# A second order table for a kernel whose instruction order, engines and PSUM banks are read from a string

## The chip, the cores and the metric

The kernel runs on one core of a Trainium2 chip. The metric is the device time in microseconds (us) of one execution. A core has a matrix engine (TensorE, PE in the profile; its weight loads are listed as PEld), a vector engine (VectorE, DVE), a scalar engine (ScalarE, ACT), a general engine (GpSimd, POOL) and a queue engine (SyncE, SP) that here only issues DMAs. Each runs its own instructions in order and waits on semaphores for the others. PE writes its results to PSUM, eight banks of 512 fp32 numbers in each of 128 partitions; DVE and ACT take them from there.

## The reference

There are four batches of 6272 time steps with 256 channels. A gated recurrence is followed by a long convolution and two gates:

```python
# first layer
sig = 1 / (1 + exp(-f_logit))
f = lower_bound + (1 - lower_bound) * sig
for t in range(6272):
    h = f[:, t] * h + (1 - f[:, t]) * x[:, t]
    y[:, t] = h
# second layer, on x = y
x1, x2, x3 = split(x @ w_proj, 3)
conv = irfft(rfft(x2, axis=1) * rfft(filter_fft, axis=0))   # length 6272
out = (x1 * conv * x3) @ w_out
```

## The kernel before, in words

The convolution of length 6272 = 49 x 128 is done with matrix products: a first transform over the 128 (F1), a second over the 49 (F2), a product with the filter's spectrum, and the two inverse steps (I2, I1). The filter's own spectrum is made once, in the head of the program, and kept in DRAM (tile H).

The kernel does not emit instructions as its Python loops run. Each loop body registers operations with `plan.op` (class Plan, L62): a kind, the engines it may run on, what it reads and writes, and a function that emits it. At the end `plan.emit` goes through a table and emits the 2413 operations in the table's order. The table is the string ORDER (L125): three characters of a 64-letter alphabet are 18 bits, and they say which operation comes next, on which engine, and in which PSUM bank a matmul operation puts its result (L99 to L106). An assertion requires that every operation comes after those it depends on. So the order on every engine's queue, the choice of engine where there is one, and the banks are data, found by a search outside the kernel.

The kinds that matter here, with the lines under which the profile shows them:

- Head (batch 0 only). The filter is loaded in 13 pieces (L630), rounded for some (fr, copies on three engines), rotated by PE (rot, rot4, L645), copied out of PSUM (f2), transformed (FF1 L672, copies afs; FF2 L690, copies hw) and stored to H (hst, L699). Small tables come from a sine on ACT (L559), ten sign instructions (signs, L547 to L557, on POOL or DVE) and scalings of the weights (W, L484). Warm-up matmuls (L610) fill PE's waits.
- Recurrence, 13 chunks of 512 steps a batch. SP loads f_logit into FL and x into XT (load, L337; batches after the first reuse three buffers of each), ACT takes a sigmoid (sig, L340), POOL multiplies (u, L342), PE turns both halves (su, L354), ACT or DVE makes f (L367, L369), DVE scans (L375). The scan of a chunk needs that of the chunk before. A wrapped copy of the early steps (wrap: POOL or ACT, or a DMA, L299) prepares a rotation.
- Projection of x2: 13 P operations (L731), each one of eight matmuls of 256 columns (one has two), and as many copies out of PSUM (x2) by ACT (L289) or DVE (L294). P needs all scans of its batch; F1 needs all x2 copies.
- Spectrum, 16 units of 8 channels a batch: F1 (L744), its copy A, a small product at the edge (mini, L760, zm), F2 (L807), the product with the spectrum from H (loads L785 into four buffers). The product is either one DVE instruction straight from PSUM (L830, called MUL in the table) or a copy (prod, L289 or L294) with the product on POOL (L839). Then slot (POOL, L812), I2 (L849) and its copy Th.
- Gate: x1 and x3 projections, 52 x13 operations a batch (L403), their copies xs, and the product z, on DVE from PSUM (L424) or on POOL (L433).
- Output: I1 (L912), which needs all Th of the batch; y (DVE, L918), which needs all z; proj (L930), its copy o, and the store (L942). It shares its time with the recurrence of the next batch.

`copy` (L286) emits the copies on whichever engine the table names, so L289 and L291 are ACT's copies, L294 and L296 are DVE's, and L301 is POOL's, whatever the operation. The tiles in the profile tell them apart.

One batch follows the other as P, spectrum with gate, output; the recurrence of the next batch is mixed in from the late spectrum on.

Of the kernel before, what the change touches and what calls it, by code (L numbers as in the profile page):

```python
# [61 lines left out]
class Plan:  # L62
# [68 lines left out]
    "gAMYD1gChKEdYCeWF5gEJYETIEygEoACdECnSEWUCoCCfOCiYCjWEXECkGEUIEVYEeSEpYE9gCuQEfCEYME8gCvAEgKEhYEiWCwUFGgEjGEkOFHg"
    "CxECpQE0ACqACrYCzSC0KEqUErEElgEuWC+QFQgCsSEvGCVgEsMEwOCyYC/ADAQE1YB2gE+AE/YFRgDBAC5UCtKFIAE2WC6EE3OE4OFJYDDQDEAE"
    "5SFagE6CFbgC3UE7KC4EFAQFDWC7YFBAFCIFkgC8UDJSFSAC9EFlgDKCFKQClgFLADCYDQUDREExYEtgCmgFTYFNSFugFcADHUDIEFEOFFOFvgDO"
    "WDPGFMIFUQFOKFPKFVAFWIFmADGgENYEZgDXUFdYDMWFXSDNGFYKFZKDLYFeQDYECWgFfADTWFhUMpgFgIDUGDWgFnYDZSFoWFiEDaCFrQF4gDxY"
    "D9YDSYFpGFwAFxYMogFjMFsADeSDfCFqODFgDgUDhEFtIFyWFzGDcSF1UF2EF0OMRgEBAMQgDdCF3MDbYC1gDiYDjQDnWF6gDoGDkIDlgGPUGQEF"
    "9SGBQGCIMqAGJWGKGGFUGGMGLQGRWF+CGMAGSGF/SGDQGEAGHUGIMGNWGOOGACMSAF7QF8AGTSGUKJNUCFgDmgJPEJOVJQNJRYJSWJUGGXQGYIGZ"
    "SJTUJVsJXVC2gMTYGbWGaCJZFGcOGVQGWADVgJYSGfgJWYJaqGogGxgJbYG6gMcgJcTJdUJeDJhVJfsJgYJiQJjFJkoGdSGeKGgWGiuGjYGpUHFQ"
    "MdgGkGGlYJmXJnSGrsGhYHGAJoHJrTJtDGqYG7QG/AHNgJpqGyWG0GGsYGmTGtsGuYHDRG1YJsWJwVGnDG2uHfgHEBJuuGvTHAYJxRG9oG+YJyFG"
    "wDJ1SG3YJzpG8YGzYJ3CHHWJ2TJ4rJ5YHJUJ0YJ6QJ7RHIGJ8IJ9pJ+YG4SHKEHLUMeAMfYG5CHMMHPYHWgHOWHSuHXQHbAJ/UHBSHYYHcYHTYJv"
    "YKARKBEHogKEXHxUHCCHQuH7gHRYHZoIEgHaYKCJKDYKGHHyEHUSHhYHgWHkuHlYHiuINgHVCHjYKFQKHAKIYH1UH2EHdSHeCHpQHtoHuYHqYHro"  # L140
    "H3UH4EMrYHzWHmSH0GH8UHnCIAsH5QIBYH+EH6IIWgH/YMUWMVGH9YMWOMYSMZCIFUMaKM0gHsYHvQIHsIIYIGYM1gIJEIKYJlYIpgHwAKJVKLFI"
    "fWIgGJqYICQIPYIDAIygIOSISCITYIQqMgWMhGIhUIiMIXQILSIYYIbAIcYM2AI7gMiOM3YIMCIZoIaYKKRMkUNAgMlMIjWIRYIUSKMBKNYIkGIl"
    "QIVCImAMmMIqWIuuKOSKPTMbgInQIoIIrYKQCKRrKSYIdUI0YIsGItYIzWI1uI2YIeEI3GMsQIvYMtAMwSMuIMvYM4UNBgNMgKTWMxCNNgMyKI4Y"
    "KUXJEgM8QNZgNYgNCAKWHKYXM5EM6MKVGKXYM9AM+IIwSIxCI9YKZWJFUKaHKbuI8SJAqNOAKdXNDYKfHJJEI5QI6AJGYKeWKguJHEI+qKiXKjTK"
    "nVKpFKoWKquKkHNEQNFAKlrKmYNIUNGINJENKMI/YNigNjgKsSKtTKuCKvrKcYJIYNPYMngNaANbYJBYJCWJDGKxSKyQKzCKwYK0oK1YK2RK3UK4"
    "BK5sNQWNUSNsgNRGK6YNSOK7QK8RNtgNkALAULBVLFWMXgK9AK+pK/YJKYLCELDtLGXNcQNfULEYN2gNVCNWKLHGLIHLJYLKWLLXNdANeILMGLNv"
    "LOYNlYKhYN3gNgENhMKrYJLSJMCNLYRsWRtQLPSLQKRuGRvALUWNmQNHgNuAMjYLVONnANoINpUOAgOBgNqENrMLRSNvYLSCLTgLWWLeQLfILZSL"
    "aKLXGNwWNzUOLgOKgN4AN5YLYgNXANxGN0ENyOLgQN1MLhALigLbSLcCLdgOCAODYLjWLkORxQLoSLpKMzYN6URzAN9WOUgOVgN7EN8MN+GN/ONT"
    "YLlQLmAOMAONYLtSLuKOEUOHQOIAOJIUvgM7ALqWLvSOFEOGMLrGLsgLyQLzIL3WL4OOOULwCLxgOPEOQMORSU7gOWAL0QL5WOSCOTKL1AL2gL6G"
    "L7gOXYOYUObQVHgOZEOaMOcAOdIU8gM/AMBWL8SL9KO0QO1AOqUOrMOmSOnCLngVIgMCOOiQOjIOsUOtEUwgOgSOhKOyWOzGU9AO2QO3AU+YVJAM"  # L150
    "DUMEMMFgOoSOkWOpKUxAOwQVKYOuUOvEOeSOxIOfCUyYL+QL/AMAgOlOMLUMMMMGWMHORwYO8SO9CRyUR0sO6QR1YO+WO4SO7AO5CMIUMJEO/OPA"
    "QPBIPDYPCSMKgPEqPFYPGqPHYPLYPKWPsgPOuPPYPMGPNYP1gPSUPUEPiQR2WR3UR7SPjAR9CR4GPIQPVYPJAR5sR8TPWsP+gPTYR+DSASPXYPQW"
    "PaQSCKPcoR/YPRGPeAPfYQHgPkTPdYSBVPmWSDtPlDPbYPYRPnGPZBPtTPxrPyYSFQSHAPvrPwYQagPoWSGRSKQR6YPpGSIBSJYSMIPgUPhEPqWP"
    "rOPuYP3YP2SP4qP5YP6CP7YQjgQIQQKAP/UQBESLTSPQSRASNrPzWQCYQAYP0GQQSQDsQsgQEYSQQSUUQRCP8WP9GQLYSSoSWMQMoQNYSVVQUSQ1"
    "gQVCSZUSbEQSWSXtUzQQTOQWSQJYU0AU1IQFUQXCQbWQduQGEU3SVTgVUgSYYQYQQfGQgYQZIQOUQlYQcYU4CQeYU5KU6gQPEQkWU/QQmGQnYU2Y"
    "VAAQtUVDSVggVfgQxEQvEVECQhVQwYQyYQouQpYSaUVBIVFKQiFQuYSeXVVASgHScsQ+QQ/AVWYQqVQ3YSfSQ2TQrNSjXShqSiYSlHREQQ4rQ5YR"
    "FARIgRAVSTYSkXSoSSpTSmvSnYRRgQ6rRjgQ7YRCQRBFSqCSrrSdYStXSuWSwORSUSsYRDARGQRHISEYRagSvHSxYRJSRWMRUEQzWRLqRNqQ0GRK"
    "YQ8QQ9ARTYRXYROYVLUVPWVsgVrgVMEVQGSOYRbQRfAVNMRMYVOgSySS0CVROVhARVYViYSzTS3RS5BRPURQERcYS1rS2YS4SS8WS+GS9RRdoRgY"
    "VXUVbWV4gV3gS/pTAYVYEReYVcGS6qS7YVZMTBQTDATCRTEpVdOVtARYSRZCTGQTIARkUVuYRosTHRTJBTKYRlYVjSVnWWBgWCgVCgVkCVlKRmEV"
    "oGTLQTMRTNAVpOTFYTOBTPYTQUTSETRVTTtVvSRpYVzQWMgWLgTUYVwCRnYVxKVqATVUTWWTXETYuTZYV0AV1ITaVTbXTfUTcFTdvTgSThETkTTm"  # L160
    "LTiqV5AV6YRhVRiFRqQRrATlUTpXTqVTjYTnsToYTrHMNSMOCTuQMPgTzWWDAWEYTstTtYV7SV8CV+UWVgV/EWNATeYTvIT0OTwQTxAWWgWAMT1W"
    "T2GWOYT4UV9KWFQT5MWGAWISaLWaMXWJCaOHWHIWKKaNGT6UT9QTygT7EVGYUCWWfgT+IWPSWXAWYYUDOWSUWQCWggWTET/QUAAWRKUEWUFGWUMU"
    "HSUIKWhAWpgUMQUNIT3gWqgT8gWZWWaGWbOWcUWzgWdEW0gWrAUJSUKCWeMWiYVSYUOQUPAWsYURWUSOWjSWmUWkCWlKV2YAcQWnEWoMdOgUBgaQ"
    "QaSAUTWUUGVmYUWQUXIUbSUcKWtUWwWWuEWvMW1AULgW2YWxGWyOUYQUZAdPgUdSUeCAiUW3QdagW4IW5IW6UW7EW8MVeYUQgUlSUmKVyAUgWUhO"
    "VaYXVQXWAXTUXUEW/QXAAXHSXICdQAdRYXBUXCMXJQXKAdbgdmgUfgUagdcAXPSXQKW9UW+MXFQXGAXLSXMKddYXRWXSGXDQXEAXNSXOKdoAUiUU"
    "jEUqQUrIaRWUGgaTuaUYXdSXeCXbQaPYXXUXYEXZWXcIaVSaWTaXKaYrXaGUnQUVgUoAXfUdngXgMXhSXjqXlCdpYXqYX5WX9GX7GXpUXrsXmYUk"
    "gYLgaaQabRadBafSXsYagTXiYacAaeYXtsXkYXuYdSWahCairdTGdWQYUgdUOXvUX+YUpgdVgX8YX6YXnSXxWYmgdXAXwEdYIaZYXzuX0YakUXoC"
    "YFSamEalQanoXyYaoYapRYGCarBYDUdzgX1uX2YYdgYEEYHSYICYBQYCIajYaqWasuauXX3UawHX4EavSYJQdZYYKIdygYMWYOuaxCdeUdiQYQGY"
    "RYatYd/gdfEdjAazSdgMYNYa0TdkIayYX/Wa1CYVUa2Da3YYAGYZsYaYYeSYPYdqWYSQYfYa4VYgCYiCa5Sa9TYXsYWYdrGYTAa6FdsOa7qa8YYh"
    "Ya/DYxQYyAYvUa+TYwEbArdhgd0AYYYYjYY1Wd1YYnQY2OYbSYcCYoYAdUYzUbBYYkWY0EYlGZCgY6SYroYsYY3UYpoY8CY5gY4MYqYY9YY7YY+q"  # L170
    "bCRbEBduWdvGdwOYtUYuEZEYZDQZHAZIYd2Sd3CZMUZQEZFoZGYZLgd+gd4KY/YZAWZNYZBGZOsZRYZPYbDRbFBbHQbIVbJAbKtZUgbGYZfWZgGZ"
    "JSZVQZKCZngbLYZXoZYYZWYd6WZZAZaYeAAd7Od8ObMUeKgZSSZTCbNVbOEeBYbRQbSRbTAZdSZeCeLgbPtbUpeWgZjWZkOeMAeNYbWQbXUbYAbb"
    "VbdNZhSZiCbZsbcRbepZoWbfYZsubQYbgQZwgZ5gbiAZtYZlSZqGZmKZrYZbUZcEbVYZyYZxQZzoZ1AbaYZ2YaCgeCWeGUehgeDGZpYZ0YeEOaDS"
    "aFCbhRblQbmSbqWbnAeHEeggbjpbsGeXgbkYbrQbvRbtAbuYboqbpYeIMbxBbwSbyqbzYZ3WZ4GaGYaEYZuQZvAaHqaIYZ6UZ8EZ9YZ+sZ/YZ7Ye"
    "FgeOWeSQeqgergePGeQOb0Sb1TeTAb2Cb3reUIeYAaJUaKEb5Sb6Wb+TeZYb7Cb8ucADb/XaAUaBEb4YcBvcCYUsQcDScFKUtAUugcETcIWcKGcG"
    "rcJUeiAcNQb9YdlYejYcHYdtYeaSebCedWe0ge1gcLseeGiqUisEirVitFesAcMYcOIeJYcPQcQAcRgecKcSSetYefOcXUekWelGenQe+gcTKcUS"
    "eoAe/ge2Ae3YcVCcYMcZUcaEemOepIccWcdOeuSevCewKexQfIgfJgeyAivUixEiwVceWiyFchScWgezIcfGeRYcbgcmUe4QfAAfBYe7WfTgciKc"
    "nMe8Ge9OcjScggfSge5AckCclge6IcoUcwWcxOcpEcrSfKAfLYfCUfFQfDEfGAcyWcsKczGc0gctSfEMcuCcvgc1Uc6WfUAfVYfHIc2MdxYfMSfP"
    "QfQAc7OfRIfNCc3Ud9Yc4EfOKc8Wc9GfWQfZUeVgfaEfbMdEWc/ScqgfXAfYIdAKd5Af0QdFOf1AfqUfiQfoSfuWfrEfpCfvGfsUftMfwSfxCfeW"
    "ffGfkUfmSfcWfnKfdOflEfgUfhMfySfjAdBQdCIdJWdKOfzCf2Sf3CiuYf8Uc5gf4Qf5Af9Mc+ggASgCqf6Wf7GizYi0Ui1VgEqgFYi2Ei5Qi7Af"  # L180
# [833 lines left out]
```

## Time and profile before

| | us |
|---|---|
| median of 3 runs (lowest to highest) | 458.27 (457.16 to 459.36) |
| the profiled execution, its own time | 459.04 |
| its span in the profile | 457.2 |
| DVE busy / ACT busy / POOL busy | 402.7 / 397.0 / 304.7 |
| PE busy (ends are modelled) / weight loads | 438.0 / 347.9 |

Seen by the first and last instructions of a kind, the profiled execution falls into these stages:

| stage | batch 0 | batch 1 | batch 2 | batch 3 |
|---|---|---|---|---|
| P starts | 71.9 | 168.8 | 269.2 | 367.3 |
| F1 starts | 84.6 | 182.7 | 282.4 | 380.0 |
| I1 starts | 144.8 | 241.9 | 339.7 | 429.8 |

FF1 of the head starts at 23.6 us and the last output copy ends at 453.7. The busy time of an engine is the union of its instructions' times; idle time of an engine that nobody waits for costs nothing. A group row of the profile gives line, engine, operation, tiles and shapes, then the count, the busy us and the mean ns of one, then the idle time just before its instructions and what ended it.

### The profile page before, as it was taken

Reading aid. Unit: us, or ns where it says so; the run is one execution under the profiler, and the core shown is the slowest. Engines: PE = TensorE matmul, PEld = TensorE weight load, DVE = VectorE, ACT = ScalarE, POOL = GpSimd, SP = SyncE. Lnnn points to the kernel's source line nnn. Section 1 sums busy time; section 2 is a strip of 40 time slices with the busy share of each in tenths; the row PEclk is TensorE's granted clock in tenths of the full one; section 3 lists DMA queues with packets and bytes.
Section 4 is the critical chain, followed back from the end, with each engine's and each line's share of the span. In section 5 each row is a group of like instructions: output and inputs, shape, how many; then the busy total and the mean of one; then the engine's idle time right before and its main releaser. Section 6 shows DMA issues by size and latency. Waiting matters only on the chain.

```text
span 457.2 us, 14624 instructions
## 1 busy us (share of the span) xinstructions
PE 438.0 (96%) x6001; PEld 347.9 (76%) x6001; DVE 402.7 (88%) x458; ACT 397.0 (87%) x564; POOL 304.7 (67%) x285
## 2 busy tenths in 40 slices
...
GB/s 325 388 351 349 337 359 342 387 192 225 304 270 277 332 332 272 179 204 288 258 289 218 273 372 253 155 312 304 247 207 285 374 97 47 239 222 154 3 322 244
DMA packets 44724, 121.02 MB, mean 265 GB/s; under 512 B 4336, under 2 KB 7920, under 8 KB 44656
## 3 DMA queue, kind: packets, MB, share of 16 engines
...
q8 instruction: 47, 0.77, 0.6%
...
## 4 chain that ended last, share of the span: by engine, by line
PE 67%; DVE 9%; ACT 9%; issue 6%; POOL 5%; DMA 3%; POOLq 0%; DVEq 0%; ACTq 0%; SPq 0%
PE PS L403 15%; PE PS L930 10%; PE PS L354 8%; PE PS L849 7%; PE PS L731 7%; PE PS L807 6%; PE PS L744 5%; DVE HA L375 4%; PE PS L912 3%; PE PS L645 2%; ACT HA L289 2%; PE PS L610 2%; DMA FL<-in_f_logit_dram 2%; POOL XT L342 2%; DMA XT<-in_x_dram 1%
## 5 line engine op out<-in xcount | busy, mean ns | idle before, releaser
L342 POOL TENSOR_TENSOR XT<-XT,FL 128x1024 f32<-128x1024 f32 (+1 forms) x49 | 110.0, 2249 | 48.9 <-ACT FL L340 46.8
L375 DVE TENSOR_TENSOR_SCAN HA<-fTs,HA,PS 128x512 f16<-128x512 f32 (+1 forms) x96 | 112.1, 1201 | 2.6 <-ACT fTs L367 1.9
L403 PE MATMUL PS<-HA,W 128*128 128x490 f16 (+1 forms) x416 | 99.8, 367 | 0.7 <-ACT XS L291 0.3
L839 POOL TENSOR_TENSOR PP<-HA,Hu 98x1008 f16<-98x1008 f16 x40 | 84.1, 2109 | 7.4 <-ACT HA L289 7.2
L289 ACT CAST HA<-PS 128x1024 f16<-128x1024 f32 (+1 forms) x102 | 80.2, 816 | 5.6 <-PE PS L744 2.8
L830 DVE TENSOR_TENSOR PP<-PS,Hu 98x1008 f16<-98x1008 f32 x56 | 66.0, 1197 | 1.4 <-PE PS L849 0.7
L918 DVE TENSOR_TENSOR ys<-PS,zt 128x1024 fp32r<-128x1024 f32 (+1 forms) x52 | 58.3, 1151 | 8.0 <-PE PS L912 3.4
L367 ACT ACTIVATE fTs<-PS,nomc 128x512 f32<-128x512 f32 (+1 forms) x92 | 59.4, 671 | 4.2 <-PE PS L354 3.3
L930 PE MATMUL PS<-Wo,ys 128*128 128x256 f32 x392 | 57.7, 293 | 1.5 <-DVE ys L918 1.3
L403 PEld LDWEIGHTS <-W 128*128 128x128 f16 x416 | 35.7, 97 | 30.4 <-issue 3.8
L291 ACT ACTIVATE XS<-PS 128x490 f32<-128x490 f32 (+1 forms) x91 | 52.2, 589 | 5.7 <-PE PS L403 3.6
L849 PEld LDWEIGHTS <-PP 98*128 98x128 f16 x1024 | 48.7, 98 | 9.7 <-POOL PP L812 2.4
L424 DVE TENSOR_TENSOR zt<-PS,XS 128x490 f16<-128x490 f32 (+1 forms) x81 | 51.5, 651 | 4.0 <-PE PS L403 1.6
L289 ACT CAST Th<-PS 128x784 f16<-128x784 f32 x63 | 51.2, 822 | 4.1 <-PE PS L849 3.6
L930 PEld LDWEIGHTS PS<-Wo,ys 128*128 128x128 f32 x392 | 49.7, 188 | 6.0 <-ACT PP L291 1.3
L433 POOL TENSOR_TENSOR zt<-XS 128x490 f16<-128x490 f32 (+1 forms) x23 | 28.0, 1223 | 39.2 <-DVE ys L918 20.6
L849 PE MATMUL PS<-VA,PP 98*128 98x98 f16 x512 | 51.9, 207 | 0.3 <-ACT HA L289 0.3
L849 PE MATMUL PS<-VB,PP 98*128 98x98 f16 x512 | 51.5, 207 | 0.0
L340 ACT ACTIVATE FL<-FL 128x1024 f32<-128x1024 f32 (+1 forms) x49 | 49.9, 1021 | 0.8 <-DMA FL<-in_f_logit_dram 0.8
L731 PE MATMUL PS<-W,HA 128*128 128x256 f16 x392 | 44.4, 273 | 1.5 <-ACT X L289 1.4
L731 PEld LDWEIGHTS <-HA 128*128 128x128 f16 x392 | 42.9, 142 | 2.4 <-issue 1.8
L354 PE MATMUL PS<-iden,FL 64*128 64x64 f32 x736 | 41.9, 230 | 2.4 <-DVE HA L375 1.3
...
## 6 DMA issues: line engine op xcount, KB each, us to landing
FL<-in_f_logit_dram SPq DMA_DIRECT2D x45, 512.0 KB, 5.6
XT<-in_x_dram SPq DMA_DIRECT2D x45, 512.0 KB, 6.2
Hu<-H SPq DMA_DIRECT2D x39, 512.0 KB, 4.5
out_dram<-osb SPq DMA_DIRECT2D x24, 512.0 KB, 4.2
out_dram<-PP SPq DMA_DIRECT2D x16, 512.0 KB, 5.1
Hl<-H SPq DMA_DIRECT2D x13, 512.0 KB, 4.7
X<-in_moe_filter_fft_dram SPq DMA_DIRECT2D x9, 512.0 KB, 7.1
out_dram<-HA SPq DMA_DIRECT2D x8, 512.0 KB, 5.5
```

Of the source, the lines that this page charges most:

```text
L289: nc.scalar.copy(dst, src)
L342: op("u", {"POOL": 0.1 + 0.553 * nb}, lambda e, xt=xt, ft=ft: nc.gpsimd.tensor_tensor(xt, xt, ft, op=AOP.mult), r=[("ft", k)], w=[("xt", k)])
L354: nc.tensor.transpose(bank(pb)[:, at[p] + j:at[p] + hn:nb], src[ps, j, cols], iden[ps, ps])
L367: nc.scalar.activation(fT, sT, AF.Identity, scale=by, bias=1.0)
L375: nc.vector.tensor_tensor_scan(h, fT, bank(pb)[:, 512 - hn:512 + hn], init, op0=AOP.mult, op1=AOP.add),
L403: nc.tensor.matmul(PS[:, p, 0:n], W13[:, kh, js], HA[:, HB[kh] + t0:HB[kh] + t0 + n], start=(kh == 0), stop=(kh == 1))
L731: nc.tensor.matmul(pp[:, r - r0, :], column(HB[kh], q_of(r)), W2[:, kh, :], start=(kh == 0), stop=(kh == 1))
L830: nc.vector.tensor_tensor(pr, px.unsqueeze(1).broadcast_to([TB, 2, UE, 63]), hh(), op=AOP.mult)
L839: nc.gpsimd.tensor_tensor(pr, spec[:, o, :, 1:64].unsqueeze(1).broadcast_to([TB, 2, UE, 63]), hh(), op=AOP.mult)
L849: nc.tensor.matmul(PS[:, ib + o, pr * TB:(pr + 1) * TB], PP[:TB, k, o, n, 2 * pr:2 * pr + 2, :], v[:TB], start=(n == 0), stop=(n == 1))
L918: nc.vector.tensor_tensor(late["ys"][:, yk, :, 0:rn * 128], PS[:, cb:cb + 2, 0:rn * 128], late["zt"][:].rearrange("p k r m -> p k (r m)") ...
L930: nc.tensor.matmul(po[:, i, :], late["ys"][:, yk, kh, i * 128:(i + 1) * 128], Wo[:, kh, :], start=(kh == 0), stop=(kh == 1))
```

## The change

Only the string ORDER is another one; every other line of the program is the same. All of its lines differ (one stretch, as an example of how it looks):

```diff
 ORDER = (
-    "BFgAAYAgQAmQAOYAhQABIApYAqgAbQAeQACIAPIAQAAVYAWYARYASIATIAUIA8gAkQAugAvAA3gDpgArQAtAA4YAsAA9SA+CBAgAzgA/CBSgAwUB"
...
+    "AqgA3gAzgAAYAOYAcQAgQBFgA4AApYAugAvYABIA8gAmQBAgAkQAiQACIAPIARIArQAsAAQAASIATIAUIA0SAtAA1CA2KBGUA5QBIEBHMA7IAwWB"
...
 )
```

Decoded, the 2413 operations are the same. 243 of them run on another engine, 589 of the 753 matmul operations write another bank, and the order differs throughout. Counts by engine, where they differ:

| operation (before -> after) | DVE | ACT | POOL | SP |
|---|---|---|---|---|
| x2 copies | 20 -> 25 | 32 -> 27 | | |
| xs copies | 19 -> 25 | 108 -> 103 | | |
| xs products (L424) / z on POOL | 81 -> 80 | | 23 -> 24 | |
| A copies | 11 -> 7 | 53 -> 57 | | |
| prod copies | 2 -> 4 | 49 -> 50 | | |
| products L830 / L839 | 77 -> 74 | | 51 -> 54 | |
| Th copies | 1 -> 3 | 63 -> 61 | | |
| o copies | 3 -> 1 | 49 -> 51 | | |
| f2 / afs / hw copies | 8, 10, 3 -> 11, 8, 5 | 18, 22, 14 -> 15, 24, 12 | | |
| fr copies | 3 -> 3 | 1 -> 2 | 3 -> 2 | |
| signs (10 instructions) | 0 -> 10 | | 10 -> 0 | |
| W scalings | | 0 -> 1 | 7 -> 6 | |
| wraps | | 7 -> 5 | 26 -> 29 | 15 -> 14 |

The program has one ACT table load more, at the head: a filter copy now stands before the sine.

Places in the order that the prediction speaks of:

```
ACT around the first P (P#0 to P#12) of batch 2
  before:  f, f, wrap | P#0 | x2#0 to #3, sig, x2#5, sig, x2#8, #10, #11, sig, o
  after:   f, f, o, sig, sig | P#0 | x2#2, #3, x2#6, sig, x2#9, #11, #12, o
DVE in P of batch 1
  before:  y | P#0 | x2#1, y, x2#3, #5, o, x2#8, #10, #12
  after:   y, y | P#0 | x2#0, #2, #3, #4, #6, #7, #10, #12
PE at the end of batch 3's spectrum
  before:  I2 (last), x13 nine times, I1 twice
  after:   x13 seven times, I2 (last), proj of batch 2, I1 four times
PE at the end of the program
  before:  proj, warm, I1, warm, proj, warm, warm
  after:   I1, I1, warm, proj, warm, warm, warm, proj, warm four times
POOL between the first and the fifth u (L342) of the head
  before:  u, mX, u, mX, mX, W, u, W four times, mX, mX, u, W, mX, W, u
  after:   u, mX, mX, u, u, mX, W, W, mX, u, mX, W, u
```

More of the change, by code (lines that the diff above doesn't have):

```diff
@@ L131 @@
[L131 to L180, printed above, removed]
@@ new lines @@
+    "BAAxOA9SA+KA/CBXgA6IBJgBKIAyOBCUBEEBYSBZKBaCBLQBMAAVYAWYAXYAYYBNABbgBcIAZWAaGBdSBeCBDEBSgBTIBUQBVABWABOgBPWBfCBQ"
+    "OBggBhYBiQBjABlYBkIBRODpgD2gBmYBpSBqKBwQBxIADgAEYDqgBuUBvMBnSB+QBzUBoKBsSBtKDrgDsADtYB5WD4AECgB0EDuUEEABrYDvMB6G"
+    "DwMDySByYB/ADzCCAWCBGD3gD5YEDgEFYD0KB3QB4AB7YCDUCEMEOgEQAAFgAIYAJYD6QB8WD7AD+SD8IB9GD/CCJUCKEEPgCCYEagEGWEHGEAKC"
+    "HQCIAERYCLYEIOCQUCREEbgEmgEngEKSELKEMKAHYEcAEdYCOQCPAESUETECSYEUMCMWCNGALYEWQEXAAGgANYEygEzgEJYCXSCYCE8gEYICeWCT"
+    "UCUMEoAEpYCfGE9gCZSCaCCbYCVgE0AE1YEeQEfIEgICgWF5gCcSChGCdCEhYEiUEjMCiYFHgEkMFGgCjWCkGEqQErACpSCnWCqCEsIE+AE/YEuU"
@@ new lines @@
+    "FRgEvMCoGCrYFQgAMACuSE2QCvKEwMCGgE3ACsWCtGE4ICwSCxCCyYE5UFagFbgE6MFIAFJYCzSFAWC0CC1gE7MFBGC5QFDSFkgFlgC6ADAUFCOD"
+    "BMFECCFgFSAAKYC3QFKWC+UC4AC8QFFKFNSFTYFLGC/EFMOCWgFugFvgDDUC9ADEEFUWDGgC7YFOKDCYDOQFPKD1YDQUEVYDxYDPIFcADRMFdYFm"
+    "AB1gFnYDHSDICDJQDKADLYElYFXUFYEDSYFVOFWOENYDTSDUCFeQFfAFZMExYFgIDMWFhSDNGD9YEtgFiCFjKDZUDaECmgFoWFpGFqOFwAFxYEZY"
+    "DgQDhAFrUFsEDXSDYCFtMDeQDbYDfAFyWFzGDiYF0OB2gDcSF1QF2AF3IDjUDkEEBYMcgDdKDnWGNQGOADoOClgC2gGBUGCEMeAF/SGACGDQGEIM"
+    "ogGHUGIMGRWGSGF4gMqADlgF7QF8AF9SF+CGFUF6gGGMDFgGJWGKOGLQGMADVgGPSGQCGTUGUMJNWJOXJSQJTRJUAJPOJQvJVJGVSGWCGZUMQgJW"
@@ new lines @@
+    "YGXWGbQGYGGcAJXSJYTGaMJcUJZKJarJeEJdVJfFDmgGdQGeIGhYGgWGiGGfgGkuGlYG7SGjYGxgGogG9CG/CDWgGqYGpUHFQHGAGrsGsYJhSJiT"
+    "JjCGtsGyWJkrMSAJlYJgYMdgJmQG6gGmRGzYG2uGnBGuYJbYGvUG+YG8YG0uG3YJnTMRgHAYJoAGwEMTYHNgJrSJtKHDQG1YHEAJsXHHUJwWHIEG"
+    "4QJprJqYJyGJuvHOSHSqHTYHJUG5AHQqHKEJxWHBQHCAJvYJ1XHRYJ3HMpgHLUHMMHPYHWgJ2TJ4rJRYHYYHXQHZoJzGJ0YHbAHaYHcYMUUMVEHU"
+    "SHVCHhYMWMMrYJ6RJ8BMfYJ7QJ9oHxWHgSHzUHyGH0EHdQHeAHqYH1WH2GHpUHfgHkqHlYHiqHjYHogHrsHtsHsYJ/TKBDHuYH3QH4AKASKCqHmW"
+    "HnGH8TH5QH6IIADH7gH+rH/YKEVKFSKGFKHqHvWIBYIFQHwGIEgIHoH9YINgIWgIJAIKYMYUM0gM1gJ+YMZEMaMIfSIgCICWIIYIPYIGYIOQISoI"
@@ new lines @@
+    "DGIQAMgSMhCIXUIbMIRYMiKIhWIiGILQIYYIZsIMAIpgKJVKLFKKWKMuM2AIjSIkCKOQKQIIygKPRKRpITYIlUIUWIVOI7gMkSNAgNBgIcYImEIn"
+    "QIoIMlCIqUIuEIsEKNYM3YIzWMsQI1GMmKMtIMuII3GKTVKVFIaYMwSNNgNMgM4WMxCMyKIrYKUUKYVIvYKWsM5GItYIdQI0YI2YM8SNYgNZgNCA"
+    "IeAM6OKZUNDYIwQI9YKaFKbsM9CI8WM+KIxAJFUJHEKIYKdQKeRKiUKjSKnTKfANOAJAuJBYKgpKhYKkEKoXKcYI+uJJEJEgNEQNPYJ5YI4YI/YK"
+    "lqKpDKqvNFANGINIUNjgNigNJEKmYKrYKsTKtSKuDKSYKXYNaANbYJCWKvqKwYJDGKxTKzDKyQNKMK0oK1YNQRNRBNSJNUWNsgNtgNVGI5UJGYI6"
+    "EJIYNWOK2QK3TKDYK4AK5rK6YNcRNdBNeJNfUJKYNgEK7QK9AK8WK+uK/YLATLCDLBXLFQLDvN2gLGRLHILEYLIpNkALKSNlYLMCLLTLNrLOYJLW"
```

58 lines of the change are left out of this document (44 added, 14 removed).

## The prediction

> **What bounds the kernel now.** I read the busy shares first, then the twelve stages of the pipeline as a table of windows, then the groups of instructions by shape, the DMA landings, and ScalarE's timeline at its table load.
>
> ```profile
> PE 438.0 (96%) x6001; PEld 347.9 (76%) x6001; DVE 402.7 (88%) x458; ACT 397.0 (87%) x564; POOL 304.7 (67%) x285
> ```
>
> PE is busiest, but matmuls overlap, so 96% overstates it. Stepping from the start of one recorded PE operation to the next and summing the tenth-percentile step of each kind gives 402 us of PE work in the 454 us to its last matmul. About 50 us are waits. The stages say who is awaited (columns: window, its length, then busy us of PE, PEld, DVE, ACT, POOL):
>
> ```profile
> core 0: us, PE busy (x) PEld busy (x) DVE busy (x) ACT busy (x) POOL busy (x), PEclk, DMA share, GB/s
> ...
> 84.60:144.80 60.20, 58.90 (x856) 41.74 (x858) 58.73 (x69) 57.15 (x89) 54.00 (x43) 1.00 0.79 268
> 144.80:168.80 24.00, 23.12 (x419) 20.36 (x419) 23.72 (x23) 22.41 (x32) 13.33 (x10) 1.00 0.95 327
> 168.80:182.70 13.90, 13.60 (x135) 13.13 (x135) 10.89 (x10) 10.42 (x11) 5.53 (x3) 1.00 0.78 279
> ...
> 269.20:282.40 13.20, 12.67 (x116) 12.05 (x113) 8.65 (x9) 11.15 (x12) 4.73 (x2) 1.00 0.83 337
> ```
>
> The first is a long stage (spectrum and gate of batch 0), the second the output stage that interleaves with the next batch's scans, the others are short stages of the x2 projection. In both PE, DVE and ACT are each above 92% of the window: three engines bound the kernel together, and the granted clock is 1.00 throughout. A table that only moves work among them can save little by load; what it changes is who waits for whom.
>
> ```profile
> L375 DVE TENSOR_TENSOR_SCAN HA<-fTs,HA,PS 128x512 f16<-128x512 f32 x88 | 108.7, 1267 | 1.9 <-ACT fTs L367 1.3
> L342 POOL TENSOR_TENSOR XT<-XT,FL 128x1024 f32<-128x1024 f32 x45 | 107.0, 2383 | 41.3 <-ACT FL L340 40.3 <-PE PS L672 0.8
> L289 ACT CAST X<-PS 128x1024 f16<-128x1024 f32 x29 | 28.9, 1038 | 9.0 <-PE PS L731 9.0
> L294 DVE CAST X<-PS 128x1024 f16<-128x1024 f32 x19 | 22.8, 1221 | 17.2 <-PE PS L731 17.2
> ```
>
> The last two rows are one operation on two engines: 1.04 us on ACT, 1.22 on DVE. They price a hand-over.
>
> **The change part by part.**
>
> *Hand-overs.* PE's work is the same. DVE gains 5 x2 copies (1.22 each), 6 x1/x3 copies (0.66), 3 filter copies (0.65), 2 of H (1.21), 2 spectrum copies (0.68), 2 of Th (0.97): 17.7 us. It loses 4 A copies (1.22), 2 filter copies L294 (0.68), 2 output copies (1.22), 3 products L830 (1.20), 1 of L424 (0.65): 12.9. Net +4.8 us. The ten sign instructions add 10 x 0.15 (rows of L529 to L534, same 128x1 shape), 1.5 us, while DVE is idle before the first filter copy: nothing. ACT sheds 4 to 5 us; POOL gains about 5.5 (3 products at 2.11, 1 of L433, 3 wraps, less the signs and two small pieces).
>
> *Where it lands.* I cut both orders at the first P, F1 and I1 of each batch and summed each engine's instructions, each at the median time until the next on its engine starts (scan 1.19, y 1.13, L830 1.12, x2 on DVE 1.21, on ACT 0.91). The busiest engine of each stage:
>
> | stage, batch 0 / 1 / 2 / 3 | before, us | after, us |
> |---|---|---|
> | F1 to I1 (DVE; batch 3 PE) | 58.3 / 54.7 / 54.2 / 46.8 | 57.7 / 55.5 / 54.9 / 47.2 |
> | I1 to next P (DVE) | 24.0 / 29.5 / 28.0 | 25.1 / 28.6 / 27.5 |
>
> That is +1.3 in the long stages and -0.3 in the output stages. It stays exposed, since the engine that would hide it is as full.
>
> *Short stages, by hand.* In batch 1 eight x2 copies instead of six go to DVE, behind two y. Twelve P at 0.87 and the copies in their order: the eighth P waits 0.8 us for its bank, the next output projection 0.6 for a copy behind a third sigmoid; F1 then starts 13.8 us after P, before 13.9. Taken as 0. In batch 2 two sigmoids come to stand on ACT ahead of P instead of behind five of its matmul groups. The first reads a load that SP can issue only when the su before has freed its buffer. From there ACT reaches the sigmoid after 0.6 (su) + 2 x 1.13 (projections) + 2 x 0.2 (short su), some 3.3 us of PE work; the shortest such distance in the order before is 5.0. The landing rows:
>
> ```profile
> FL<-in_f_logit_dram SPq DMA_DIRECT2D x45, 512.0 KB, 5.6
> XT<-in_x_dram SPq DMA_DIRECT2D x45, 512.0 KB, 6.2
> Hu<-H SPq DMA_DIRECT2D x39, 512.0 KB, 4.5
> ```
>
> So ACT stands until about 2.4 us into P, two sigmoids end at 4.4, the third x2 copy at 5.4, and the sixth P waits 1.1 us; F1 starts after 13.05 us, before 13.2. Taken as 0; with the 7.57 us that one FL transfer took in the chain of waits, +2.0. In batch 0 one more x13 stands before F1: +0.4.
>
> *Late loads.* Before P of batch 3 two loads have 4.4 and 5.0 us of PE work ahead of their sigmoid (shortest before in that stretch: 5.9), and two spectrum loads of batch 3 have 4.1 and 4.2 us (shortest before: 5.2) against 4.5 landing and about 0.4 of issue. Late by 0.6 to 1.6, some of it behind other work: I take +1.0 in all (bounds 0 and 2.6).
>
> *Head.* Up to the fifth chunk POOL has 12.9 us of work after the first L342 instead of 16.4, because the weight scalings L484 are spread out. The chain of waits runs through POOL there (L342 and four L484 from 26 to 45 us), and DVE is busy only 19.76 of 22.8 us in the window 22.9 to 45.7. At most those 3.0 us come back; after that DVE is full (22.22 of 22.9), and its work to P falls by 0.7. I take -1.5 (bounds -3.0 and 0).
>
> ACT also loads a third table there, because a copy now precedes the sine:
>
> ```profile
> 23.57 1.28 ACT L340 ACT_TABLE_LOAD   x1
> 24.86 1.06 ACT L340 ACTIVATE FL<-FL 128x1024 f32<-128x1024 f32 x1
> ```
>
> One more costs 1.28 us, during which ACT waits for filter matmuls anyway: nothing; uncovered, +1.3. [...]
>
> *Tail.* The last I2 now stands behind all x13, so its Th (0.82) is awaited before the first I1: y starts 2.3 us after the last x13 instead of 0.95, with 1.0 us of other PE work inside: +0.3. Three warm matmuls before the last projection take the place of two and an I1: 0.
>
> Sum: 1.3 - 0.3 + 0.4 + 0 + 0 + 1.0 - 1.5 + 0.3 = **+1.2 us**. The profiled execution took 459.04 (span 457.2 and 1.8 around it), so 460.2; the median of the runs is 458.27, 0.77 less, so **459.5**.
>
> **The rivals.**
>
> A, the head gives all and the loads land in time. For it: DVE's idle time lies exactly where POOL's queue is shortened, and median landings hide quick ones. Against: loads reuse four buffers, and late input would hold the scans as POOL does now. -0.3 - 3.0 with the long stages even: 455.0.
>
> B, DVE becomes the bound in every stage, and each microsecond given to it is paid: +4.8, plus the late loads at 1.0, and nothing from the head: 464.1. Place: x2 of batches 1 and 2 and the long stages; price 1.22 us for each x2. It decides once DVE's share of a long stage passes PE's; the windows have 58.73 against 58.90. [...] The trace does not settle it.
>
> C, the order moves nothing measurable, waits change places only: 458.3 within 1.
>
> That the change does other than it says is excluded by counts: the same 2413 operations stand in both orders, 243 of them on another engine.
>
> **How the numbers follow.** Forecast 0.40 (457.5 to 462, of which 0.12 beyond 460.6), A 0.25, B 0.27, C 0.08. The 0.5% that a measurement of this kernel can tell is 2.3 us: below 456.0 faster, above 460.6 slower. Faster 0.24 (A, less 0.01), same 0.28 + 0.08 + 0.01 = 0.37, slower 0.12 + 0.27 = 0.39. The range goes from A less the 1.1 us by which the runs before scatter, 453.9, to B with the same, 465.2.
>
> **What would show it.** P of batch 0 starting 1 to 2 us earlier than 71.9, and POOL's L342 starting sooner in the head. ACT's sigmoid L340 waiting for the FL transfer near P of batch 2 (before: 0.8 us in all). Long stages of 57 to 61 us with DVE's busy time up by under 1 us each. Idle time of DVE's L830 in batch 3 put down to the Hu transfer. For B: PE waits released by DVE growing, most of all P by the x2 copies L294. The forecast is wrong if the head keeps its 71.9 or loses 3, or if a long stage moves by over 2 us with loads this equal: then round trips between engines, which I have not priced one by one, decide.

## The result and the profile after

The changed kernel takes 461.24 us (median of 22 runs, 458.94 to 464.07), the kernel before 458.26 (22 runs beside them): a ratio of 1.0064, 95% interval 1.0046 to 1.0082. It is slower by 0.64%, 3.0 us, where 1.2 were forecast. The profiled execution took 461.20, its span 459.3 (before 459.04 and 457.2).

The busy shares (first line) and the stages (columns as in the prediction):

```profile
PE 440.5 (96%) x6001; PEld 349.2 (76%) x6001; DVE 407.8 (89%) x476; ACT 392.4 (85%) x557; POOL 308.7 (67%) x280
```

```profile
core 0: us, PE busy (x) PEld busy (x) DVE busy (x) ACT busy (x) POOL busy (x), PEclk, DMA share, GB/s
...
85.00:144.70 59.70, 59.07 (x854) 41.82 (x852) 58.53 (x73) 56.83 (x86) 54.49 (x41) 1.00 0.82 278
144.70:168.60 23.90, 23.39 (x421) 20.52 (x421) 23.78 (x23) 22.66 (x33) 13.72 (x11) 1.00 0.86 304
168.60:182.00 13.40, 12.48 (x125) 12.13 (x124) 11.80 (x11) 8.82 (x10) 5.87 (x3) 1.00 0.67 259
...
269.20:281.50 12.30, 12.30 (x115) 11.85 (x112) 10.31 (x9) 9.33 (x11) 6.97 (x3) 1.00 0.89 311
...
339.40:368.30 28.90, 26.48 (x481) 23.20 (x480) 27.36 (x27) 24.13 (x33) 15.05 (x10) 1.00 0.63 223
```

DVE has 5.1 us more work (402.7 to 407.8; counted were 4.8, and 1.5 for the sign instructions) and ACT 4.6 less. The four short stages from P to F1 have 5.1 us more DVE work in sum and got shorter, batches 1 and 2 (168.60 and 269.20) from 13.9 and 13.2 to 13.4 and 12.3. The last row is the output stage ahead of P of batch 3, 28.9 us. The same stage before took 27.6, with DVE 0.2 us less busy and ACT 1.2 more:

```profile
339.70:367.30 27.60, 26.64 (x481) 23.16 (x480) 27.19 (x27) 25.34 (x36) 15.69 (x12) 1.00 0.86 309
```

Stage by stage, after less before, in us:

| | batch 0 | batch 1 | batch 2 | batch 3 | sum | forecast |
|---|---|---|---|---|---|---|
| start to P (head) | +0.7 | | | | +0.7 | -1.5 |
| P to F1 | -0.3 | -0.5 | -0.9 | 0.0 | -1.7 | +0.4 |
| F1 to I1 (long) | -0.5 | +0.4 | +0.6 | +1.0 | +1.5 | +1.3 |
| I1 to next P (output) | -0.1 | +0.3 | +1.3 | | +1.5 | -0.3, and +1.0 for late loads |
| I1 to the end | | | | +0.1 | +0.1 | +0.3 |

The sum is 2.1 us, the difference of the spans. The other 0.8 between this and the 3.0 of the medians is that the execution profiled before lay 0.8 above its median, and the one after at its median. Part of why that median is high: 9 of the 22 runs have a mean granted clock of 0.993 to 0.996, with a median of 462.9 us; the 13 at 1.00 have 460.4.

The groups that the prediction priced, and ACT's sigmoid:

```profile
L375 DVE TENSOR_TENSOR_SCAN HA<-fTs,HA,PS 128x512 f16<-128x512 f32 x88 | 109.9, 1271 | 5.3 <-ACT fTs L367 4.7
L342 POOL TENSOR_TENSOR XT<-XT,FL 128x1024 f32<-128x1024 f32 x45 | 106.7, 2379 | 44.5 <-ACT FL L340 23.5 <-PE PS L354 12.4 <-DMA XT<-in_x_dram 7.3
L340 ACT ACTIVATE FL<-FL 128x1024 f32<-128x1024 f32 x45 | 47.5, 1061 | 3.9 <-DMA FL<-in_f_logit_dram 3.6
L294 DVE CAST X<-PS 128x1024 f16<-128x1024 f32 x22 | 26.3, 1230 | 9.3 <-PE PS L731 9.3
L289 ACT CAST X<-PS 128x1024 f16<-128x1024 f32 x26 | 25.7, 1019 | 12.5 <-PE PS L731 12.5
```

The copies cost what they did. New are the two waits for loads: 7.3 us of POOL for XT and 3.6 us of ACT for FL (before: none, and 0.8). POOL's lie in P of batch 2 and cost nothing there. ACT's longest are in the stage that grew (ACT's waits from 350 to 362 us):

```profile
ACT FL L340 <- DMA FL<-in_f_logit_dram: 1.4, 1, 1.4
...
ACT osb L291 <- DMA out_dram<-osb: 0.4, 1, 0.4
```

The landing rows of the whole run hide this: their medians stand as before or below it (FL 5.6 before). The rows of 349 to 361 us alone follow in the second fence:

```profile
FL<-in_f_logit_dram SPq DMA_DIRECT2D x45, 512.0 KB, 5.5
XT<-in_x_dram SPq DMA_DIRECT2D x45, 512.0 KB, 5.9
```

```profile
FL<-in_f_logit_dram SPq DMA_DIRECT2D x1, 512.0 KB, 6.4
XT<-in_x_dram SPq DMA_DIRECT2D x1, 512.0 KB, 7.5
out_dram<-osb SPq DMA_DIRECT2D x1, 512.0 KB, 7.9
```

The two orders in the windows 349 to 361 and 361 to 367 us, first before, then after (the last two columns are the share of the DMA engines and GB/s):

```profile
349.00:361.00 12.00, 11.94 (x214) 10.55 (x212) 12.00 (x11) 11.13 (x16) 6.18 (x4) 1.00 0.93 343
361.00:367.00 6.00, 5.26 (x105) 4.60 (x100) 5.74 (x7) 4.96 (x9) 1.84 (x3) 1.00 0.94 369
```

```profile
349.00:361.00 12.00, 10.49 (x202) 9.30 (x197) 10.91 (x10) 9.81 (x12) 6.91 (x3) 1.00 0.95 336
361.00:367.00 6.00, 5.64 (x80) 4.54 (x80) 5.94 (x6) 5.21 (x10) 1.49 (x3) 1.00 0.06 21
```

Both keep the DMA engines busy for over nine tenths of the first window, and the changed order moves no more in it (336 against 343 GB/s). In the second window they stay full before and stand idle after. PE, DVE and ACT are each busy 1.1 to 1.5 us less in the first window. So the amount does not explain the stall; which transfer stands ahead of which, and who needs it when, is tested below.

### The profile page after: what moved, and what is told of

Same layout as the page of the kernel before. It is cut to its first block, busy times and chain, and to the rows that moved or that the text cites. A ratio compares the mean times of both kernels' runs of the same rounds, so it can differ in the third digit from the quotient of the medians.

```text
span 459.3 us, 14584 instructions
## 1 busy us (share of the span) xinstructions
PE 440.5 (96%) x6001; PEld 349.2 (76%) x6001; DVE 407.8 (89%) x476; ACT 392.4 (85%) x557; POOL 308.7 (67%) x280
## 4 chain that ended last, share of the span: by engine, by line
PE 63%; DVE 15%; ACT 9%; issue 6%; DMA 5%; POOL 2%; SPq 0%; DVEq 0%; ACTq 0%; POOLq 0%
PE PS L403 14%; PE PS L731 9%; PE PS L930 7%; PE PS L849 6%; PE PS L354 6%; DVE HA L375 6%; PE PS L807 5%; PE PS L744 4%; DVE ys L918 4%; DMA FL<-in_f_logit_dram 3%; PE PS L912 3%; PE PS L672 2%; PE PS L645 2%; ACT HA L289 2%; DMA out_dram<-osb 2%
## 5 line engine op out<-in xcount | busy, mean ns | idle before, releaser
L375 DVE TENSOR_TENSOR_SCAN HA<-fTs,HA,PS 128x512 f16<-128x512 f32 (+1 forms) x96 | 113.4, 1204 | 5.7 <-ACT fTs L367 4.7
L289 ACT CAST HA<-PS 128x1024 f16<-128x1024 f32 (+1 forms) x107 | 84.1, 823 | 6.6 <-PE PS L744 2.8
L839 POOL TENSOR_TENSOR PP<-HA,Hu 98x1008 f16<-98x1008 f16 x41 | 86.0, 2105 | 0.8 <-ACT HA L289 0.4
L830 DVE TENSOR_TENSOR PP<-PS,Hu 98x1008 f16<-98x1008 f32 x55 | 64.7, 1199 | 3.7 <-ACT HA L289 0.9
L433 POOL TENSOR_TENSOR zt<-XS 128x490 f16<-128x490 f32 (+1 forms) x24 | 29.3, 1223 | 44.2 <-DVE ys L918 21.3
L424 DVE TENSOR_TENSOR zt<-PS,XS 128x490 f16<-128x490 f32 (+1 forms) x80 | 50.8, 649 | 3.5 <-ACT XS L291 1.5
L289 ACT CAST Th<-PS 128x784 f16<-128x784 f32 x61 | 49.9, 825 | 4.4 <-PE PS L849 3.6
L291 ACT ACTIVATE XS<-PS 128x490 f32<-128x490 f32 (+1 forms) x82 | 47.6, 588 | 6.8 <-PE PS L403 4.6
L340 ACT ACTIVATE FL<-FL 128x1024 f32<-128x1024 f32 (+1 forms) x49 | 49.2, 1010 | 3.9 <-DMA FL<-in_f_logit_dram 3.6
```

Source lines behind the costliest of these rows:

```text
L289: nc.scalar.copy(dst, src)
L375: nc.vector.tensor_tensor_scan(h, fT, bank(pb)[:, 512 - hn:512 + hn], init, op0=AOP.mult, op1=AOP.add),
L830: nc.vector.tensor_tensor(pr, px.unsqueeze(1).broadcast_to([TB, 2, UE, 63]), hh(), op=AOP.mult)
L839: nc.gpsimd.tensor_tensor(pr, spec[:, o, :, 1:64].unsqueeze(1).broadcast_to([TB, 2, UE, 63]), hh(), op=AOP.mult)
```

## The experiments

In most of these kernels the table takes two lines less, so their line numbers are 2 lower than above (L338 is the sigmoid L340). Medians and ratios to the kernel before, run beside them (458.2 to 458.6 us):

| run | us | ratio, 95% interval |
|---|---|---|
| head_of_before | 470.28 | 1.0255 (1.0226 to 1.0285) |
| middle_of_after | 467.27 | 1.0193 (1.0172 to 1.0215) |
| head_of_after | 460.52 | 1.0048 (1.0033 to 1.0064) |
| late_of_before | 460.43 | 1.0046 (1.0029 to 1.0064) |
| sigmoid_later | 460.55 | 1.0050 (1.0029 to 1.0070) |
| quarter_loads_after | 456.92 | 0.9957 (0.9935 to 0.9979) |
| quarter_loads_before | 457.12 | 0.9965 (0.9951 to 0.9978) |
| sine_first | 460.16 | 1.0047 (1.0027 to 1.0067) |
| store_earlier | 459.37 | 1.0011 (0.9995 to 1.0028) |
| x2_back_to_act | 461.84 | 1.0083 (1.0055 to 1.0111) |
| head_of_before_later_cut | 461.94 | 1.0080 (1.0059 to 1.0101) |
| four_mends | 460.01 | 1.0033 (1.0015 to 1.0052) |

### Splicing the two orders

Each part of one order was put together with the rest of the other; an operation that one part has already done is dropped from the next.

```
head_of_before   order before up to the first P of batch 0, then the changed one
middle_of_after  before up to that P, changed up to F1 of batch 2, then before
head_of_after    changed up to the first P of batch 0, then before
late_of_before   changed up to F1 of batch 2, then before
```

> The order of before up to the first P of batch 0, the order of after from there. Theory 1 (the losses lie in the second half: 1.3 us before P of batch 3, 1.0 in the last long stage, 0.6 behind the last copy, and the head loses about 0.7): 460.5 us, P of batch 0 at 71.9 instead of 72.6. Rival (the head's 0.7 is scatter between executions): 461.2.

> The order of before up to the first P of batch 0, of after from there to the first F1 of batch 2, of before from there. Theory 1 (by the stage times of the two profiles the middle of after is 1.6 us shorter): 456.7 us, faster than both. Rival (what a stage gains is given back by the next, as waits change places): 458.3 us.

> The order of after up to the first P of batch 0, the order of before from there. Theory 1: 459.0 us, P of batch 0 at about 72.6. Rival (scatter): 458.3 and P near 71.9. If the head had given the 1.5 that the prediction took: 456.8.

> The order of after up to the first F1 of batch 2, the order of before from there. Theory 1 (the loss of 3 us lies behind that point, and the middle of after is 1.0 to 1.6 ahead of before): 457.5 to 458.3 us. Rival (the loss goes with the work handed to VectorE, 1.2 us a copy, three of the five x2 copies and half of the others before that point): 459.8 us.

No theory's time came out, and the cuts themselves cost. In head_of_before and middle_of_after P to F1 of batch 0 takes 21.5 us instead of 12.7. The waits of head_of_before from 71 to 98 us, and its windows around the stall:

```profile
ACT FL L338 <- DMA FL<-in_f_logit_dram: 7.8, 1, 7.8
...
PE PS L729 <- ACT X L287: 6.6, 1, 6.6
```

```profile
78.00:82.00 4.00, 1.59 (x15) 1.47 (x14) 1.42 (x2) 0.00 (x0) 0.00 (x0) 1.00 1.05 410
82.00:86.00 4.00, 0.00 (x0) 0.00 (x0) 0.00 (x0) 1.86 (x3) 0.00 (x0) 0.79 1.04 391
86.00:90.00 4.00, 3.85 (x19) 2.99 (x19) 0.24 (x1) 3.78 (x5) 0.00 (x0) 0.50 0.62 238
```

One sigmoid stands ahead of the x2 copies, while its load, issued at 73.45 among the stores of H, takes 10.7 us to land. It stops ACT for 7.8 us and PE for 6.6, and the clock falls behind it (0.79, then 0.50): it is the prediction's late sigmoid, with 8.8 us more in the stage. The DMA engines are full through the stall (shares 1.05 and 1.04).

What lies away from the cuts can still be read. In late_of_before the stage ahead of P of batch 3 is back at 27.6 us and the last long stage at 49.7 (changed: 28.9 and 50.8), as its theory expected. Its time is the rival's within the interval (459.5 to 461.1, expected 459.8), but not for the rival's reason: P of batch 2 starts at 269.2, as before, so in sum nothing was lost up to there. What it lost lies in P to F1 of batch 2, where the cut is (13.9 instead of 12.3), and in the end (28.9 instead of 27.4). head_of_after has its theory's sign and more than its size: 2.4 us above the kernel before, where 459.0 was expected. In its profile P of batch 0 starts 1.4 later and the long stage behind the cut is 0.5 longer, so head and cut are not told apart.

### Light loads

```diff
-                    dst, src[b, t0:t0 + n, :].rearrange("(p j) d -> p j d", p=128)),
+                    dst[0:32 if b else 128], src[b, t0:t0 + n, :].rearrange("(p j) d -> p j d", p=128)
+                    [0:32 if b else 128]),
```

> The changed order, with the loads of f_logit and x of batches 1 to 3 bringing 32 of 128 partitions (three quarters of these rows are left out; everything else is computed on what the buffers hold). Theory: late input is what makes the stage ahead of P of batch 3 long, so it comes back to 27.3 to 27.9 us, the sigmoids wait under 0.5 us for FL in all (3.6 us in the changed kernel), no run has a mean clock under 0.997, and the time is 458.0 to 459.5 us. The head, whose loads are whole, and the last long stage stay as they are. Rival: the order itself, not the loads, makes the stage long: 28.4 us or more, 460.5 to 461.5 us.

> The order before, with the loads of f_logit and x of batches 1 to 3 bringing 32 of 128 partitions (three quarters of these rows are left out). Theory: its sigmoids waited 0.8 us for FL in all, so there is little to win: 457.4 to 458.3 us. Rival: smaller loads speed everything that moves data, and this kernel gains as the changed one does: 1.5 us or more, 456.8 us or less.

The changed order gains 4.3 us on its 461.24, the one before 1.1 to 1.5, and the two end level (456.92 and 457.12). So the net loss of the change goes with these loads; with them light, the new order with its fuller DVE is no slower. The stage ahead of P of batch 3, changed order with light loads:

```profile
337.20:364.80 27.60, 26.75 (x482) 23.27 (x481) 27.21 (x27) 24.16 (x33) 15.01 (x10) 1.00 0.40 141
```

The theory held on the stage, and the time fell even below its range. The last long stage stayed at 50.7 us: that 1.0 is the order's own. For the kernel before, 457.12 lies between its two expectations, 0.3 below the theory's range and 0.3 above the rival's.

### One wait behind the other

```diff
 ACT, output stage ahead of P of batch 3
-  f, sig, f, o, o
+  f, f, o, sig, o
```

> The changed order, with one sigmoid of batch 3 (and the product on POOL that takes it) put behind the next output copy on ACT; in the changed kernel this sigmoid is the one that starts at 357.21 after 1.37 us of waiting for its FL load. Theory: that load is the stall ahead of P of batch 3, and the stall costs twice: the stage from I1 of batch 2 to P of batch 3 is 28.9 us instead of 27.6, and PE is busy for only 54% of the 3.4 us from 357.8 (no other such stretch before the last projection is under 70%), after which the clock falls in some runs: 9 of the 22 runs of the changed kernel have a mean granted clock of 0.993 to 0.996, with a median of 462.9 us, against 460.4 for the 13 at 1.00. Then the stage comes back to 27.3 to 27.9 us, at most one of six runs has a mean clock under 0.997, and the time is 458.7 to 459.7 us (461.24 less 1.3, less the 0.8 by which the median lies above that of the runs at full clock). Rival: the wait shows there but something behind it is as late (the store of an output buffer, landed at 360.03, that the next output copy needs): the stage stays at 28.4 to 28.9 us, two or three of six runs have the lower clock, 460.7 to 461.5 us.

The rival was right on the stage, which stayed at 28.9 us; the time, 460.55, is just under its range. ACT no longer waits for FL there, but for as long before the output copy:

```profile
ACT osb L289 <- DVE ys L916: 1.4, 1, 1.4
```

The profile names DVE's y as releaser. That copy starts at 359.41, though, and the store that holds its buffer landed at 359.31: a copy into osb has to wait for it. In the changed kernel this store's data are ready at 343.98, and SP issues it here, behind two pairs of loads (SP's timeline):

```profile
349.74 0.34 SPq L942 DMA_DIRECT2D out_dram<-PP  x1
350.81 0.33 SPq L337 DMA_DIRECT2D FL<-in_f_logit_dram  x1
351.23 0.87 SPq L337 DMA_DIRECT2D XT<-in_x_dram  x1
352.15 0.42 SPq L942 DMA_DIRECT2D out_dram<-osb  x1
```

So the next run moves the store as well:

```diff
 SP, same stage (the sigmoid as in sigmoid_later)
   store osb
+  store osb
   load, load, store PP, load, load
-  store osb
```

> The changed order with two moves in the output stage ahead of P of batch 3: the sigmoid behind the next output copy as in sigmoid_later, and one store of an output buffer, whose data are ready at 343.98 us and which is issued at 352.15 behind two pairs of loads in SP's order, put ahead of both pairs. Theory: what stalls there is the queue of transfers as the changed order bunches them; moving the sigmoid alone left ACT's next output copy waiting until 359.4 for the store of its buffer, which landed at 359.31. With the store early too, both are in time: the stage is 27.3 to 28.0 us instead of 28.9, PE is busy for over 70% of every 3.4 us there, at most one in eight runs has a mean clock under 0.997, and the time is 458.6 to 459.7 us. Rival: any transfer made earlier makes another late, since the queue is full (share 0.91 to 0.99 from 349 to 361 us): the stage stays at 28.4 us or more and the time at 460.0 us or more.

The theory held in all its numbers. The stage, and the transfers from 349 to 361 us:

```profile
339.80:367.30 27.50, 26.61 (x481) 23.20 (x480) 27.11 (x27) 24.07 (x33) 15.01 (x10) 1.00 0.66 238
```

```profile
FL<-in_f_logit_dram SPq DMA_DIRECT2D x1, 512.0 KB, 5.0
```

The load lands in 5.0 us instead of 6.4, the store is out of the way by 350.8, and the stage is back. The DMA engines still stand idle behind it (share 0.10 from 361 to 367 us), so it was the order of the transfers that stalled the stage. Two moved operations of ACT and SP (and the POOL product that goes with one) take the loss from 3.0 us to 0.5 (by the ratio) or 1.1 (by the medians, 459.37 against 458.25), and none of 12 runs has the lower clock. The store was not moved alone: the sigmoid in its old place had 5.0 us of lead, about what the load now takes, so that might have been enough.

### The head, and DVE

```diff
 ACT, start of the program
-  fr, f2, sine
+  sine, fr, f2
```

> The changed order, with the sine on ACT put back ahead of the first filter copy, which takes one of the three ACT table loads (1.28 us) away. By the prediction the third load was hidden: the first filter matmul of the scans stays at 23.6 to 24.3 us (the three profiles with the changed head have 23.8, 24.1 and 24.3) and the time is 460.7 to 461.7 us. Rival: in the head ACT's filter copies are what is awaited, and the load is on the path: that matmul starts at 22.5 to 23.2 us and the time is 459.8 to 460.4 us.

The time, 460.16, is the rival's; FF1 starts at 23.3 instead of 23.8, between the two ranges. ACT's first instructions (start, us), in the changed kernel and here:

```profile
5.59 1.05 ACT L289 CAST afs<-X 128x1024 fp32r<-128x1024 f32 x1 [3.59 <-DMA X<-in_moe_filter_fft_dram]
7.76 0.65 ACT L289 CAST f<-PS 128x512 fp32r<-128x512 f32 x1 [1.13 <-PE PS L645]
8.43 1.28 ACT L559 ACT_TABLE_LOAD   x1
```

```profile
0.71 1.28 ACT L557 ACT_TABLE_LOAD   x1 [0.71 <-PEq L996]
6.32 0.47 ACT L557 ACTIVATE PP<-PP 128x324 f32<-128x324 f32 x1 [4.32 <-DVE PP L523]
6.70 1.03 ACT L287 CAST afs<-X 128x1024 fp32r<-128x1024 f32 x1
```

The third table load stands between the first copies, not in idle time. Over all the profiles, FF1 starts at 23.7 to 24.3 us with the changed head (seven), at 23.3 and 23.7 with the sine first, and at 23.0 to 23.6 with the head before (five). P of batch 0, in the profiles that are not cut there, starts at 71.6 to 73.6 with the changed head (six, mean 72.6), at 70.6 and 71.6 with the sine first, and at 71.5 to 71.9 with the head before (three).

> The changed order with four x2 copies handed back from DVE to ACT (the fourth and eighth of batch 1, the fifth and eighth of batch 2): DVE loses 4 x 1.22 = 4.9 us, ACT gains 4 x 1.04 = 4.2 us. Forecast of the prediction (hand-overs in the short stages cost nothing, PE hides them): 460.7 to 461.8 us, P to F1 of batches 1 and 2 within 0.5 us of 13.4 and 12.3. Rival B (DVE is the bound, each copy given to it is paid): 456.2 to 457.5 us, and each of these stages shorter by 1 to 2.4 us.

461.84 us, just above the forecast's range and 4.3 above the top of rival B's. The stage of batch 2 stayed at 12.3. That of batch 1 became longer, 1.3 us where the forecast allowed 0.5 and B wanted it shorter (changed: 13.40 with DVE 11.80 and ACT 8.82):

```profile
168.50:183.20 14.70, 12.62 (x125) 12.15 (x124) 9.45 (x9) 10.76 (x12) 7.05 (x3) 1.00 0.63 243
```

DVE had room; PE waits 1.1 us in this stage for an x2 copy on ACT, which it did not in the changed kernel.

### Two that did not come out

head_of_before_later_cut takes the order before until F1 of batch 0 has begun; four_mends is sine_first and store_earlier together, with the order before from F1 of batch 3.

> The order before until F1 of batch 0 has begun (602 of 2413 operations), then the changed order. The cut lies where the two orders have done nearly the same operations (11 differ), so that no sigmoid stands far ahead of its load, as it did in head_of_before, where one waited 7.8 us. Theory: the changed head costs 1.3 to 2.2 us (P of batch 0 at 72.4 to 73.3 instead of 71.9; the changed head with the rest of before took 460.52 against 458.17), so without it 459.0 to 460.2 us. Rival: what the head gains or loses is taken up again in the next stages, because the batch that follows waits for its input anyway: 460.7 us or more.

> The changed order with the sine first, the sigmoid later, the store earlier, and the order before from F1 of batch 3 on (cut where 8 operations differ). Theory: sine first 460.2 in an own run; the stall ahead of P of batch 3 another 0.8 us, the clock that follows it 0.8, the last long stage 1.0 (50.8 us against 49.8), the end 0.5: 456.4 to 458.0 us, below the 458.3 of the kernel before, with the last long stage at 49.6 to 50.1 us. Rival: each mend gives way to another late transfer, as moving the sigmoid alone did: 458.8 to 460.3 us.

Both theories missed, and both times lie in their rivals' ranges. The first has its head (P at 71.5) but loses 2.0 us in the long stage of batch 0, where DVE is busy for only 4.44 of the 6 us from 114, and another 1.0 ahead of P of batch 3, where ACT waited 2.6 us for FL. The second gets 27.6 us ahead of P of batch 3, but 52.0 in the last long stage (before 49.8): just behind the cut DVE is busy 3.63 of 6 us, before 6.00. No wait for a transfer is listed in that stage, so it is not the late transfer of its rival. No mixture beat both kernels, and none of the full computations is shown to be faster than the kernel before.

## Why the prediction was right or wrong

The time lies in the range and the sign was right, but it is above 460.6, the prediction's line for slower, and 1.8 us of the 3.0 were missed. That no more was missed is partly luck: the head came out 2.2 us worse than its term and the short stages 2.1 better, and the two nearly cancel. Of the mechanisms, late transfers are the one that the runs bear out.

**Long stages, +1.3:** the size came out, +1.5, and nearly by batch too (-0.6, +0.8, +0.7, +0.4 counted; -0.5, +0.4, +0.6, +1.0 measured). Its reason did not: the term took DVE's queue as the limit, and DVE's busy time in these stages fell, by 0.2, 0.4, 0.7 and 0.5 us, while PE's rose. Batches 2 and 3, before and after:

```profile
282.40:339.70 57.30, 57.26 (x833) 42.11 (x833) 55.64 (x66) 54.73 (x86) 52.46 (x43) 1.00 0.73 246
380.00:429.80 49.80, 49.46 (x640) 34.91 (x638) 47.02 (x62) 41.79 (x61) 32.79 (x32) 1.00 0.50 152
```

```profile
281.50:339.40 57.90, 57.84 (x832) 41.88 (x830) 54.98 (x67) 55.64 (x85) 51.41 (x45) 1.00 0.73 254
381.00:431.80 50.80, 50.27 (x640) 35.41 (x640) 46.49 (x63) 41.41 (x61) 37.94 (x35) 1.00 0.43 139
```

The changed order has two x13 operations more in batch 2's stage and one more in batch 3's, which fits PE's rise but was not tested. Batch 3 gained most, 1.0. late_of_before undoes that and light loads do not, so it is order; which of its moves is open.

**Hand-overs and rival B:** B is refuted. DVE's 5.1 us more are not paid: the short stages that hold them got shorter, with light loads the two orders are level, and giving copies back did not make it faster (461.84 against 461.24, within the noise of the two). Neither DVE's total busy time nor PE's decided.

**Short stages, +0.4 and 0:** too high; they gave 1.7 us. In P of batch 2 FL landed at 269.66, as ACT came to it at 269.68, so ACT did not stand at all. More x2 copies on DVE shortened the stage of batch 1, as x2_back_to_act shows; in batch 2 two copies given back changed nothing, so what made that stage 0.9 shorter is open.

**Late loads, +1.0:** the mechanism was right, the term too small and half in the wrong place. Of the two FL loads ahead of P of batch 3 the one with 5.0 us of lead was late by 1.4; no spectrum load of batch 3 was. The error was to hold each lead against the median landing of 5.6: where the queue is full a load took 6.4, a store 7.9. Before the change an FL load of 128 KB took 6.7 us in the same stretch, and ACT did not wait for it, since its sigmoid came later. And only loads were looked at. The store that kept an output buffer was as late, and hid behind the sigmoid.

**Head, -1.5:** failed, +0.7 here and about +0.9 over the profiles. POOL's gain was there: the sixth and seventh chunks' scans end at 51.2 and 54.3 us instead of 52.5 and 56.8. But the tenth's end at 66.2 in both. The stretch from the seventh chunk's scans to P, before and after:

```profile
56.80:71.90 15.10, 13.26 (x194) 10.88 (x192) 14.87 (x17) 14.71 (x25) 11.10 (x15) 1.00 1.00 329
```

```profile
54.30:72.60 18.30, 17.22 (x228) 13.60 (x228) 16.63 (x19) 17.02 (x29) 17.04 (x21) 1.00 1.01 364
```

It takes 3.2 us more. DVE has 1.8 us more to do in it: three filter copies (afs, 1.9 us) stand there, where DVE had none of them before, and FF1 (L672) has 44 matmuls left instead of 32. Part of the gain was filter work put off, where the prediction had DVE's work to P fall by 0.7. The other 1.4 is idle time of DVE behind ACT, and ACT waits for loads, as it did nowhere there before (the changed kernel's waits from 44 to 72.6 us):

```profile
ACT FL L340 <- DMA FL<-in_f_logit_dram: 1.3, 2, 0.7
...
ACT XS L340 <- DMA XS<-in_f_logit_dram: 0.7, 1, 0.7
```

With the sine first these two waits are 0.3 in all (0.9 in four_mends), that stretch takes 17.0 us, and P starts 0.6 earlier than before on the mean: so much of the 1.5 may have been to be had. That earlier work meets its loads was the objection that the prediction held against rival A, and left out of its own sum.

The other step that failed is the third table load, "during which ACT waits for filter matmuls anyway: nothing". It stood between copies, and FF1 came later with it. Taking it out gave 1.5 us at P (means of 72.6 and 71.1, the second of two profiles 1 us apart) and 1.1 in the medians, whose intervals overlap (1.0027 to 1.0067 and 1.0046 to 1.0082). Both are near the 1.28 of the table load's row, which the prediction named as the uncovered price.

**Tail, +0.3:** right within what one profile shows (+0.1).

**The clock:** not in the prediction. Of the kernels that stall ahead of P of batch 3, the changed one, sigmoid_later, sine_first and x2_back_to_act have 9 of 22, 2 of 9, 4 of 12 and 2 of 6 runs at a mean of 0.993 to 0.996; store_earlier, four_mends and both light-load kernels, without the stall, have none of 38, the kernel before 1 of 56. In the changed profile PE is busy for 2.39 of the 4 us from 357.5, against at least 2.74 in every 4 us from 25 to 452 us that lie apart from these. That ties the clock to the stall, but does not show it: the clock of that profile reads 1.00 there. None of these kernels' profiled executions was such a run; head_of_before_later_cut, whose stall is deeper, has none in 6; and in store_earlier, with none in 12, PE waits in the head (59 to 67 us) for as long as ahead of P of batch 3 in the changed kernel, 1.3 us.
